# A new lead-in, loads in another order and one explicit emission order, in a kernel of layernorm, local attention and feed-forward

## The chip, the cores and the metric

One core of one Trainium2 chip. The metric is the device time of one execution in microseconds (us). Differences here are about one per cent, so each kernel was run several times beside runs of the kernel before on the same chip. Not all calls ran on the same chip, and there is one trace of each run. "Span" is the time from the first to the last record of the one execution that was profiled; it is about 2 us shorter than that execution's device time.

## The reference

A block of 2048 rows of 640 numbers: layernorm, then attention and feed-forward beside each other, all added to the input. Each row attends to 8 rows, itself and 7 earlier ones two apart.

```python
xn = _layernorm(x)
# attention: 32 heads of 20; logits over 8 offsets 0, 2, ..., 14 back
qkv = (xn @ wqkv) ...
logits = einsum("bhsd,bhswd->bhsw", q, kg) * scale      # kg: 8 shifted copies of k
o = einsum("bhsw,bhswd->bhsd", softmax(logits), vg)
# feed-forward 640 -> 1536 -> 640
h = gelu(xn @ w1 + b1)
return x + o @ wo + (h @ w2 + b2)
```

## The kernel before

The rows are cut into four chunks of 512, a chunk into four blocks of 128. Products with weights run on TensorE. The elementwise q times k and attention times v run on VectorE (32 passes of each, 1.48 us a pass). ScalarE empties TensorE's accumulator banks ("evictions") and does gelu and exp. Every piece of work has a name: `st10` is the statistics of chunk 1, block 0; `rs1` the root for all of chunk 1; `hc..`, `gc..` and `pc..` evict q, k, v; `qk..` are products of q and k, `lg..` the logits, `xs`/`xd` the DMAs that spread the attention weights (tile `ax`), `av..` their products with v, `ot` their sum, `f1`/`ge` the feed-forward with its gelu, `o...` output products, `oc`/`od` their eviction and the add into the output in memory. Each engine runs its pieces in the order in which they are emitted.

In the kernel before, that order comes out of a small greedy model that is run while the kernel is built:

```python
for eng in (PE, VE, SE, DQ):            # the plan's clock moves on; each free engine takes
    best = None                         # the ready piece of the lowest rank
    for t in left:
        if any(n not in end or end[n] + ... > now for n in t["needs"]):
            continue
        if any(len(held[p]) + k > self.pools[p] for p, k in new.items()):
            continue
        best = t
    ...
for t in make_plan(fns).run():          # pieces in order of their planned start
    t["fn"]()
```

Of the kernel before, what the change touches and what calls it, by code (L numbers as in the profile page):

```python
# [10 lines left out]
ACT = mybir.ActivationFunctionType  # L11
# [4 lines left out]
PE, VE, SE, DQ = "pe", "ve", "se", "dq"  # L16


class Plan:
# [8 lines left out]
    LAG = {PE: 0.22, VE: 0.08, SE: 0.1, DQ: 0.0}  # L28
# [4 lines left out]

    def pool(self, name, n):
        self.pools[name] = n

    def add(self, name, engine, us, rank, needs, fn, bufs=(), after=0.0, table=None, slack=0.0):
        t = {
            "name": name,
            "eng": engine,  # L40
            "us": us,
            "rank": rank + self.offsets.get(name[: 4 if name[:2] in ("pj", "pc", "ad") else 3], 0.0),
            "needs": list(needs),
            "fn": fn,
            "bufs": list(bufs),
            "after": after,
            "table": table,
            "slack": slack,
            "i": len(self.tasks),
        }  # L50
        self.tasks.append(t)
        self.by[name] = t
        for b in bufs:
            self.bufs.setdefault(b, set()).add(name)
        return name

    def run(self):
        end, left, held = {}, list(self.tasks), {p: {} for p in self.pools}
        remaining = {b: set(u) for b, u in self.bufs.items()}
        free = {PE: 0.0, VE: 0.0, SE: 0.0, DQ: 0.0}  # L60
        now, started, table = 0.0, [], "sqrt"
        running, slacks = [], {t["slack"] for t in self.tasks}
        while left:
            done = [t for t in running if t["end"] <= now + 1e-9]
            for t in done:
                running.remove(t)
                for b in t["bufs"]:
                    remaining[b].discard(t["name"])
                    if not remaining[b]:
                        held[b[0]].pop(b, None)  # L70
            moved = True
            while moved:
                moved = False
                for eng in (PE, VE, SE, DQ):
                    if free[eng] > now + 1e-9:
                        continue
                    best = None
                    for t in left:
                        if t["eng"] != eng or t["after"] > now + 1e-9:
                            continue  # L80
                        if best is not None and (t["rank"], t["i"]) >= (best["rank"], best["i"]):
                            continue
                        if any(
                            n not in end
                            or end[n] + t["slack"] + (self.LAG[self.by[n]["eng"]] if self.by[n]["eng"] != eng else 0.0) > now + 1e-9
                            for n in t["needs"]
                        ):
                            continue
                        new = {}
                        for b in t["bufs"]:  # L90
                            if b not in held[b[0]]:
                                new[b[0]] = new.get(b[0], 0) + 1
                        if any(len(held[p]) + k > self.pools[p] for p, k in new.items()):
                            continue
                        best = t
                    if best is not None:
                        left.remove(best)
                        best["start"], best["end"] = now, now + best["us"]
                        if best["table"] not in (None, table):
                            table = best["table"]  # L100
                            best["end"] += self.TABLE
                        end[best["name"]] = best["end"]
                        free[eng] = best["end"]
                        for b in best["bufs"]:
                            held[b[0]][b] = True
                        running.append(best)
                        started.append(best)
                        moved = True
            nxt = [f for f in free.values() if f > now + 1e-9]
            for late in slacks:  # L110
                ready = [e + late + self.LAG[self.by[n]["eng"]] for n, e in end.items()]
                nxt += [r for r in ready if r > now + 1e-9]
            nxt += [t["after"] for t in left if t["after"] > now + 1e-9]
            if left and not nxt:
                raise RuntimeError("no piece can start: " + ", ".join(t["name"] for t in left[:8]))
            if left:
                now = min(nxt)
        return started
# [3 lines left out]
P = 128  # L122
# [8 lines left out]
EPS = 1e-5  # L131
MASKED = -1e9
# [4 lines left out]
GROUPS = (((0, 0, 4),), ((1, 0, 4),), ((0, 4, 5), (1, 4, 5)), ((2, 0, 4),), ((2, 4, 5),))  # L137
# [3 lines left out]
RANK = {  # L141
    "av1": 36.4, "av2": 74, "f12": 4.1, "f13": 69.4, "gj1": 19.4, "gj2": -19.4, "o02": -8.9, "o10": 15.3,
    "o12": -3.3, "o13": -11.3, "o20": 117, "o31": 57.5, "o33": 85.2, "ot0": 20, "pj22": -106.4, "pj31": -13.1,
    "qk1": -4.8, "qk2": 4.4, "st2": 164.2, "st3": 219.3, "xn0": -14.7,
}


def make_plan(fns, offsets=RANK):

    pl = Plan(offsets)  # L150
    for name, n in (
        ("acc", 4), ("L", 1), ("O", 1), ("xnT", 3), ("q", 2), ("k", 2), ("v", 2), ("prod", 4),
        ("e", 1), ("attn", 1), ("ax", 1), ("oT", 1), ("hT", 18), ("osb", 2), ("xn", 2), ("m", 1), ("rs", 1), ("ss", 1),
    ):
        pl.pool(name, n)
# [3 lines left out]

    def done(n, which):  # L160
        if n:
            return [f"pc{n}{which}{to}" for to in range(KT)]
        return [f"gc{bl}{g}" for bl in range(BPC) for g, parts in enumerate(GROUPS) if which in [p[0] for p in parts]]

    pl.add("b1", VE, 0.1, -90, [], f("b1"), after=21.0)
    for n in range(NCH):
# [6 lines left out]
        for bl in range(BPC):  # L173
            land = (4.0, 4.0, 9.6, 9.6)[bl] if n == 0 else (0.0, 13.3, 17.1, 17.1)[n]
            r = -40 if n else -99
            pl.add(f"st{n}{bl}a", VE, 0.5, r, [], f("st", n, bl, 0), after=land)
            pl.add(f"st{n}{bl}", VE, 0.62, r, [f"st{n}{bl}a"] + ([f"rc{n}{bl - 1}"] if n == 0 and bl else []), f("st", n, bl, 1))
            if n == 0:
                pl.add(f"rs{n}{bl}", SE, 0.35, -99, [f"st{n}{bl}"], f("sqrt", n, bl, bl + 1), table="sqrt")
                pl.add(f"rc{n}{bl}", VE, 0.17, -99, [f"rs{n}{bl}"], f("rstd", n, bl, bl + 1))  # L180
# [3 lines left out]
        for bl in range(BPC):  # L184
            xn, tp = ("xn", n, bl), ("acc", "tp", n, bl)
            if n > 0:
                pl.add(f"xn{n}{bl}", SE, 0.81, early + -4.0, [f"rc{n}"], f("xn", n, bl), [xn])
                pl.add(f"tc{n}{bl}", DQ, 4.0 if n > 1 else 2.7, early - 3.0, [f"xn{n}{bl}"], f("td", n, bl), [xn, xnT], 21.5)
                continue

            for i, (a, b) in enumerate(((0, 2), (2, KT)) if bl == 0 else ((0, KT),)):
                u = "a" if b < KT else ""
                us = (b - a) / KT
                pl.add(f"xn{n}{bl}{u}", VE, 0.06 + 0.36 * us, -99, [f"rc{n}{bl}"], f("xn", n, bl, a, b), [xn])
                pl.add(f"tp{n}{bl}{u}", PE, (0.54 if bl == 0 else 0.3) * us, -99, [f"xn{n}{bl}{u}"], f("tp", n, bl, a, b), [xn, tp])
                pl.add(f"tc{n}{bl}{u}", SE, 0.16 + 0.49 * us, -99, [f"tp{n}{bl}{u}"], f("tc", n, bl, a, b), [tp, xnT])
        if n == 1:
            pl.add("ld", DQ, 9.2, -1000, [f"tc1{bl}" for bl in range(BPC)], f("ld"))
        pl.add(f"xp{n}", DQ, 0.3, base + 30, ["ld"], f("xp", n))
        pl.add(f"xb{n}", DQ, 0.0, base + 33, [f"xp{n}"], f("xb", n))  # L200

        if n == 0:
            for bl in range(BPC):
                for g, parts in enumerate(GROUPS):
                    ps, last = ("acc", "g", bl, g), max(p[0] for p in parts)
                    tos = sum(p[2] - p[1] for p in parts)
                    land = (6.4, 8.7, 11.8)[last]
                    r = -50 + (last == 2)
                    need, cut = [f"tc0{bl}"], 0
                    if bl == 0 and g == 0:  # L210
                        cut = 2
                        need.append(pl.add("ga00", PE, 0.112 * tos, r, ["tc00a"], f("gj", bl, g, 0, cut), [xnT, ps], land))
                    pl.add(f"gj{bl}{g}", PE, 0.056 * (KT - cut) * tos, r, need, f("gj", bl, g, cut, KT), [xnT, ps], land)
# [544 lines left out]
```

## Time and profile before

| what | before |
|---|---|
| device time, median of 3 (range) | 215.14 us (214.96 to 215.17) |
| span of the profiled execution | 212.4 us |
| first real product on TensorE | 7.03 us |
| last product done | 209.65 us |
| from there to the end ("tail") | 2.75 us |
| VectorE, ScalarE busy | 82%, 52% |

Read it as three stretches: up to the first product, the time in which TensorE is nearly always busy, and the tail. The profile's lines are in the prediction below. In this trace TensorE waits once for another engine after its filler, 0.46 us just before the first product.

### The profile page before, as it was taken

How to read it: one execution, taken by the hardware profiler on the slowest of the kernel's cores; microseconds unless marked ns; L12 is line 12 of the kernel's file. 1: busy time of each engine (PE TensorE's matmuls, PEld its weight loads, DVE VectorE, ACT ScalarE, POOL GpSimd, SP SyncE). 2: the span in 40 equal slices, each digit the busy share in tenths (PEclk: the TensorE clock that was granted, in tenths of full speed). 3: DMA queues.
4: the chain of work that ended last, by engine and by line, in shares of the span. 5: the costliest groups of instructions: out<-in, count | busy, mean ns of one | idle time of the engine just before them, and what ended most of it. 6: DMA issues, size and time to landing. Idle time of an engine off the chain costs nothing.

```text
span 212.4 us, 3961 instructions
## 1 busy us (share of the span) xinstructions
PE 206.9 (97%) x1670; PEld 121.7 (57%) x1693; DVE 174.4 (82%) x178; ACT 109.5 (52%) x193; POOL 19.7 (9%) x37
## 2 busy tenths in 40 slices
PE   8999999999999999999999999999999999999994
PEld 8799845655545555555555555455555455555552
DVE  3579999759999997599996999999999999972001
ACT  3568997798574654931353883503752511341120
POOL 2000000000020024101100010101110011101130
PEclk9999999999999999999999999999999999999999
DMA  6999528916829199993120027202114611122214
GB/s 216 365 362 376 93 50 275 322 24 132 206 64 163 37 287 196 197 195 89 15 30 0 0 31 200 31 3 31 14 21 48 180 19 22 27 29 31 34 16 76
DMA packets 23465, 23.95 MB, mean 113 GB/s; under 512 B 9112, under 2 KB 20632, under 8 KB 23448
## 3 DMA queue, kind: packets, MB, share of 16 engines
q1 hardware_dynamic: 17864, 16.49, 28.3%
q0 software_dynamic: 4144, 4.92, 17.2%
q10 hardware_dynamic: 1440, 2.29, 3.9%
q8 instruction: 13, 0.21, 0.4%
q14 instruction: 4, 0.03, 0.1%
HBM read 10.00 MB, written 7.54 MB: 83 GB/s over the span
## 4 chain that ended last, share of the span: by engine, by line
PE 97%; issue 1%; DVE 0%; ACT 0%
PE lo L684 27%; PE hps L653 24%; PE pps L484 23%; PE gps L501 8%; PE hi L686 8%; PE L L557 4%; PE idle L725 2%; PE tp L437 1%; ACT xnT L441 0%; DVE osb L714 0%; DVE zeros L361 0%
## 5 line engine op out<-in xcount | busy, mean ns | idle before, releaser
L653 PE MATMUL hps<-xnT,w_sb 128*128 128x512 bf16 x235 | 54.1, 379 | 0.3
L684 PE MATMUL lo<-w_sb,hT 128*128 128x512 bf16 x183 | 51.8, 379 | 0.0
L631 DVE TENSOR_TENSOR pv<-vT,ax 128x2560 bf16<-128x2560 bf16 x32 | 45.9, 1484 | 1.7 <-PE L L557 1.7
L535 DVE TENSOR_TENSOR prod<-qT,kT 128x2560 bf16<-128x2560 bf16 x32 | 45.4, 1484 | 0.0
L686 PE MATMUL hi<-w_sb,hT 128*128 128x128 bf16 x192 | 40.3, 219 | 0.6 <-issue 0.2
L664 ACT ACTIVATE hT<-hps,b1T 128x512 bf16<-128x512 f32 x48 | 31.6, 687 | 17.0 <-PE hps L653 13.3
L653 PEld LDWEIGHTS <-w_sb 128*128 128x128 bf16 x240 | 23.0, 98 | 26.7
L640 DVE TENSOR_TENSOR pv<-pv 128x5120 bf16<-128x5120 bf16 x12 | 33.9, 2825 | 0.4
L684 PEld LDWEIGHTS <-hT 128*128 128x128 bf16 x192 | 18.7, 98 | 22.8 <-issue 0.6
L691 ACT CAST osb<-lo 128x512 bf16<-128x512 f32 x15 | 8.8, 585 | 44.0 <-issue 28.0
L697 POOL DMA_DIRECT2D out_dram<-osb x15 | 12.9, 863 | 110.5 <-ACT osb L692 110.5
L684 PE MATMUL lo<-wo,oT 128*128 128x512 bf16 x79 | 23.0, 379 | 0.0
L686 PEld LDWEIGHTS <-hT 128*128 128x128 bf16 x192 | 18.4, 98 | 1.5
L398 DVE BATCH_NORM_STATS2 stats<-x_sb 128x6 f32<-128x320 bf16 x32 | 14.0, 469 | 5.1 <-DMA x_sb<-in_A_x_dram 5.1
L484 PE MATMUL pps<-xnT,wq_sb 128*128 128x512 bf16 x71 | 16.9, 380 | 0.2
L484 PE MATMUL pps<-xnT,wv_sb 128*128 128x512 bf16 x73 | 16.9, 379 | 0.1
L686 PE MATMUL hi<-wo,oT 128*128 128x128 bf16 x80 | 16.9, 219 | 0.1
L484 PE MATMUL pps<-xnT,wk_sb 128*128 128x512 bf16 x73 | 16.8, 379 | 0.1
L705 DVE TENSOR_TENSOR osb<-lo,x_sb 128x512 bf16<-128x512 f32 x1 | 0.7, 692 | 16.1 <-PE lo L684 16.1
L520 ACT CAST qT<-pps 128x512 bf16<-128x512 f32 x15 | 8.8, 585 | 9.2 <-PE pps L484 9.2
L684 PEld LDWEIGHTS <-oT 128*128 128x128 bf16 x80 | 7.8, 98 | 9.4
L484 PEld LDWEIGHTS <-wk_sb 128*128 128x128 bf16 x75 | 8.7, 118 | 7.3 <-issue 0.2
(62 smaller groups left out, 205.9 us busy)
## 6 DMA issues: line engine op xcount, KB each, us to landing
w_sb<-in_B_w_dram SPq DMA_DIRECT2D x2, 1920.0 KB, 9.2
out_dram<-osb POOLq DMA_DIRECT2D x15, 160.0 KB, 3.4
ax<-attn SPq DMA_DIRECT2D x8, 256.0 KB, 5.4
ax<-attn ACTq DMA_DIRECT2D x8, 256.0 KB, 5.6
out_dram<-x_sb SPq DMA_DIRECT2D x3, 640.0 KB, 4.3
out_dram<-b2bc POOLq DMA_DIRECT2D x3, 640.0 KB, 8.2
x_sb<-in_A_x_dram SPq DMA_DIRECT2D x1, 1280.0 KB, 13.3
wq_sb<-in_A_wqkv_dram SPq DMA_DIRECT2D x1, 800.0 KB, 4.8
```

The costliest lines, as they stand in the source:

```text
L398: nc.vector.bn_stats(stats[:, i, :], x_sb[:, b, i * (D // 2) : (i + 1) * (D // 2)])
L484: nc.tensor.matmul(ps[:], lhsT=wqkv_p[which][:, ti, to, :], rhs=xnT[:, ti, :], start=(ti == 0), stop=(ti == KT - 1),)
L501: nc.tensor.matmul(ps[:, i, :], lhsT=wqkv_p[which][:, ti, to, :], rhs=tiles["xnT", 0][:, ti, cs], start=(ti == 0 and (i == 0 or b == KT an ...
L520: nc.scalar.copy(dest[:, to, off : off + CH], tiles["pps", n, which, to][:])
L535: nc.vector.tensor_tensor(out=prod[:, i, :, :], in0=qkv_tile(n, 0)[:], in1=qkv_tile(n, 1)[:, :, off : off + CH], op=ALU.mult,)
L631: nc.vector.tensor_tensor(out=pv[:, i, :, :].rearrange("p t (j c) -> p t j c", j=BPC), in0=qkv_tile(n, 2)[:, :, off : off + CH].rearrange( ...
L640: nc.vector.tensor_tensor(out=ta[:], in0=ta[:], in1=tb[:], op=ALU.add)
L653: nc.tensor.matmul(ps[:], lhsT=w1_sb[:, ti, ft * P : (ft + 1) * P], rhs=tiles["xnT", n][:, ti, :], start=(ti == 0), stop=(ti == KT - 1),)
L664: nc.scalar.activation(hT[:], tiles["hps", n, ft][:], ACT.Gelu_apprx_tanh, bias=b1T[:, ft : ft + 1], scale=1.0)
L684: nc.tensor.matmul(lo[:], lhsT=lhs, rhs=rhs[:, 0:CH], start=first, stop=last)
L686: nc.tensor.matmul(hi[:, 0 : D - CH], lhsT=lhs, rhs=rhs[:, CH:D], start=first, stop=last)
L697: nc.gpsimd.dma_start(rows, tiles["osb", n, bl][:], accum_op=ALU.add)
```

## The change

Its intent is to start TensorE's real work earlier and to replace the greedy order by one that was searched offline. Block 0 is loaded alone, block 1 a little later (its load waits for a tiny fill on VectorE); block 1's statistics move to ScalarE; q, k and v of chunk 0 are made for pairs of blocks, 256 columns at a time (q of the first pair stays at 128); the transposed copies are shared between VectorE and ScalarE. w1 is loaded in two halves ahead of the last x. And the order of all pieces is one fixed list. Smaller edits are not shown, among them that the filler products read a constant and so start at 0.78 and not 0.99 us, and that the statistics get four buffers and not two. The core of the diff, cuts marked:

```diff
-    for cs in (slice(BPC, 2 * BPC), slice(2 * BPC, NCH * BPC)):
-        nc.sync.dma_start(x_sb[:, cs, :], x_nb[:, cs, :])
-    nc.sync.dma_start_transpose(b1_t[:], b1_rt[:])
-    nc.sync.dma_start(w1_sb[:], B_w1.rearrange("(t p) n -> p t n", p=P))
+    load_x(0, 1)
+    nc.vector.memset(x_sb[:, 1, 0:16], 0.0)
+    nc.scalar.dma_start(x_sb[:, 1, :], x_nb[:, 1, :])
...
+    load_x(BPC, 2 * BPC)
+    for c in range(2):
+        cs = slice(c * F // 2, (c + 1) * F // 2)
+        nc.sync.dma_start(w1_sb[:, :, cs], w1_v[:, :, cs])
+    nc.sync.dma_start_transpose(b1_t[:], b1_rt[:])
+    load_x(2 * BPC, NCH * BPC)
...
+    def do_sum1():
+        nc.scalar.activation(trash()[:], x_sb[:, 1, :], ACT.Identity, accum_out=acc1[:])
+    def do_sq1():
+        nc.scalar.activation(trash()[:], x_sb[:, 1, :], ACT.Square, bias=neg1[:], scale=RD, accum_out=mv[:, 1, 1:2])
...
+    def do_gp(which, pair, a, b):            # was: one block, 128 columns
+        for to in range(a, b):
+            for ti in range(KT):
+                nc.tensor.matmul(ps[:, to - a, :], lhsT=wqkv_p[which][:, ti, to, :],
+                    rhs=tiles["xnT", 0][:, ti, pair * 2 * P : (pair + 1) * 2 * P], ...)
...
+ORDER = """
+pad01 pad02 st00a st00 sm rs00 me nm rc00 sq xn00a xn00b tp00a tp00b tc00a rs01 ga tc00b rc01 xn01 gb2 tp01 gb3
...
+xn03 hc101 st12a tp02 st12 tp03 tc02 hj201 st10a tc03 st11a hj202 st11 hc200 hj010 st13a hc202 st13 hj011 st10 rs1
+hj110 hc010 rc1 hc011 hj112 xn10 hj111 hc112 hc110 hj012 xn11 hj210 hc012 hc111 st31a hj211 st22a hc210 tc11 qk020
+f107 hc211 hc201 b1 st20a f101 ge07 qk001 ...
...
+o233 ad31 ge31 o234 ge35 o330 oc23 o310 ad30 od23 o300 od13 o331 o301 ad32 o332 o302 o311 o312 ot3 o313 o303 o304
+o314 oc30 od30 o320 oc31 o321 od31 o322 o323 o324 o333 oc32 o334 od32 ohi oclo ochi
+""".split()
...
-        for t in make_plan(fns).run():
-            t["fn"]()
...
+        for name in ORDER:
+            pieces[name]["fn"]()
```

## The prediction

> **What bounds the kernel now.** I read the page first, then busy time by stretch, then TensorE in order of time over the first 25 us and the last 10, and last what VectorE and ScalarE did before TensorE's first real product. The page, its span, its engine row, and the chain that ended last:
>
> ```profile
> span 212.4 us, 3961 instructions
> ...
> PE 206.9 (97%) x1670; PEld 121.7 (57%) x1693; DVE 174.4 (82%) x178; ACT 109.5 (52%) x193; POOL 19.7 (9%) x37
> ...
> PE 97%; issue 1%; DVE 0%; ACT 0%
> ```
>
> TensorE carries 97% of the chain, so time can come only from TensorE doing less, starting earlier, or ending nearer the last byte. "Busy" isn't "at its peak", so I cut the span where TensorE's own timeline says its role changes: first real product at 7.03, first feed-forward product at 24.86, last product done at about 209.65. In the view of busy time by stretch (stretch, its length, PE busy, PEld, DVE, ACT, POOL, clock, DMA share, GB/s):
>
> ```profile
> 0.00:7.03 7.03, 5.58 (x49) 5.08 (x50) 2.98 (x10) 2.21 (x5) 1.46 (x18) 1.00 0.76 253
> 7.03:24.86 17.83, 17.83 (x315) 17.62 (x315) 14.26 (x43) 13.74 (x35) 0.00 (x0) 1.00 0.97 317
> 24.86:209.65 184.79, 183.46 (x1309) 99.03 (x1330) 156.90 (x125) 93.50 (x156) 18.21 (x19) 1.00 0.45 88
> 209.65:212.40 2.75, 0.00 (x0) 0.00 (x0) 0.29 (x1) 0.00 (x0) 0.00 (x0) 1.00 0.20 60
> ```
>
> The body, 184.79 us, is what a better order could fill. Is it already full? Starts of neighbouring matmuls in this trace lie 0.2158 us apart at 512 columns and 0.0558 at 128. The body holds 240 feed-forward and 225 projection matmuls of 512 (465 x 0.2158 = 100.3), 272 output pairs of 512 and 128 (272 x 0.2716 = 73.9), and the logits: one group of 80 at 2.30 us and six of 40 at 1.20 (9.5). That is 183.7, so about 1 us is left in 184.79, and most of it is the hand-over into and out of the narrow logits tiles (about 0.1 each, 14 times), which any order has. Order alone can win almost nothing here; it can only lose. What remains is the first 25 us. TensorE there (start, length, engine, line, what):
>
> ```profile
> 0.99 4.87 PE L725 MATMUL idle<-zeros 128*128 128x128 bf16 x44 [0.99 <-DVE zeros L361]
> 5.80 0.77 PE L437 MATMUL tp<-ident,xn 128*128 128x128 bf16 x5
> 7.03 1.28 PE L501 MATMUL gps<-xnT,wq_sb 128*128 128x128 bf16 x20 [0.46 <-ACT xnT L441]
> ...
> 22.07 2.95 PE L501 MATMUL gps<-xnT,wv_sb 128*128 128x128 bf16 x50
> 24.86 1.46 PE L653 MATMUL hps<-xnT,w_sb 128*128 128x512 bf16 x5
> ```
>
> The 44 products of zeros are filler; work begins at 7.03. What it waits for, on VectorE and ScalarE:
>
> ```profile
> 3.71 0.89 DVE L398 BATCH_NORM_STATS2 stats<-x_sb 128x6 f32<-128x320 bf16 x2 [2.77 <-DMA x_sb<-in_A_x_dram]
> 4.87 0.30 ACT L404 ACTIVATE std<-mv,eps_t 128x1 f32<-128x1 f32 x1 [2.18 <-DVE mv L400]
> 6.61 0.75 ACT L441 COPY xnT<-tp 128x256 bf16<-128x256 bf16 x2 [1.44 <-PE tp L437]
> 19.84 0.93 ACT L420 ACTIVATE xn<-x_sb,nmr,rstd 128x640 bf16<-128x640 bf16 x1
> x_sb<-in_A_x_dram SPq DMA_DIRECT2D x1, 160.0 KB, 2.9
> x_sb<-in_A_x_dram ACTq DMA_DIRECT2D x1, 160.0 KB, 3.1
> ```
>
> The reader is to see a chain of small steps: landing 3.68, statistics 3.71, root 4.87, first product 7.03. It is 3.32 us from landing to product and 2.16 from root to product. The fourth line is there only as the price of one ScalarE pass over a 640-wide block.
>
> **What the Trainium skill says.** "TensorE: Matmul & The Clock Gate", section "Back-to-back issue gap", gives N/2.4 + 2.5 ns per warm matmul: a fixed part beside the columns. The trace agrees: 50 products of 128 take 24.86 - 22.07 = 2.79 us, 55.8 ns each. By the same formula one of 256 takes 109.2 ns, against 111.6 for two of 128. The same page, Part 1 ("The HAM clock gate"), says that the array starts at half clock and needs about 3.4 us of work. Here the filler still ran at 107 ns a start up to 5.5 us, and the products at 7.03 at 56, so the filler is needed and its length barely suffices. "DMA: Bandwidth & Descriptors", section "Issuing engines are not separate DMA queues", says that loads from different engines share the same 16 engines and interleave. The trace agrees: the first two x loads, issued together, landed together, 2.9 and 3.1 us after issue.
>
> **The change, part by part.**
> (1) Block 0 alone first. The load of block 1 now waits for a tiny VectorE fill (in the kernel before, VectorE's first fill ran at 0.82 to 0.94), so it is issued near 1.05 and not 0.75. Block 0 has the engines to itself for that 0.3 us. I estimate that it lands 0.3 earlier, at 3.35, and block 1 at about 3.95 and not 3.86.
> (2) Block 1's statistics go to ScalarE: a sum pass, a negated mean, a square pass. In ScalarE's order the sum pass stands before block 0's root. It costs about 0.8 to 0.9 (the 0.93 row, less overlap). If block 1 lands at 3.6 the pass ends at about 4.4, when the statistics of block 0 are just done (3.35 + 1.16 = 4.5), and the root starts at 4.5. If block 1 lands at 3.95, the root starts at about 4.85, where it was. So the first product comes at 4.5 + 2.16 = 6.66 or at about 7.0. The first copy of the transposed block moves to VectorE, which frees the second for ScalarE at the same time; that is worth 0.1 at most for the products after the first ten. I take 6.6 for the first product: a gain of 0.4.
> (3) Pairs of blocks. The 300 lead-in products of 128 become 50 of 128 and 125 of 256: the same columns and 125 fewer matmuls. 50 x 0.0558 + 125 x 0.1092 = 2.79 + 13.65 = 16.44, against 300 x 0.0558 = 16.74: 0.3 saved, all on the bound engine.
> (4) The stretch from 7.03 holds 17.83 us, of which 16.74 are products and 15 transposes are 0.84. About 0.25 are small stalls. The new sequence keeps one such place (the first halves of block 1 wait for the VectorE copy), so I count 0.1 won.
> (5) Loads of w1 in halves before x of the last two chunks, and the order of output adds: all of it is off TensorE's path (w1 landed at 23.16 before, just ahead of its use at 24.86; now earlier). 0.
> (6) The end. Before, 17 products of 512 and 17 of 128 follow the last full block (3.67 + 0.96 us); now part of them is done earlier and only 8 of 512 and 17 of 128 follow (1.73 + 0.95). The last GpSimd add was issued about 1.04 after its block ended and landed 3.58 later, so it now lands about 1.9 to 2.0 us after TensorE's end, where the last small store landed 1.84 after it. I count 0.1 lost.
> (7) The fixed order in the body: 0, with the risk below.
> Sum: 0.4 + 0.3 + 0.1 - 0.1 = 0.7 us won of 215.14, so 214.4.
>
> **The rivals.**
> (a) Block 1 delays block 0: the sum pass holds the root, and after the root the square pass holds the other half of block 0's transposed copy. For it: ScalarE runs in order, and only 0.1 to 0.4 us of room is there. Against it: nothing but the small size of the delay. Then (1) and (2) give 0 or even -0.3, and the time is 214.8 to 215.2.
> (b) The fixed order stalls TensorE in the body. Tightest is the last attention chunk. By sums of trace durations, its logits end near 162 us; maximum, subtraction, exponential, sums, reciprocal and product (1.2 + 1.2 + 1.06 + 1.4 + 0.95 + 1.22, with hand-overs 7.2) bring 169.2; spreading the weights takes up to 6.3, 175.5; eight products of 1.43, three additions of 2.82 and the last addition of 1.49 bring 196.9. TensorE asks for it near 198.6. So there are some 1.7 us of room, where the kernel before had its result at 192.7 and asked for it at 195.89: 3.2 us. A late stage would cost a stall of its lateness. For it: VectorE is 82% busy. Against it: at every other place that I summed the room is 2 us or more. This would make 214.5 to 216.
> (c) The lead-in meets the landings: key weights landed at 8.59 and value weights at 11.75 before; the new order asks for them at about 10 and 12.7. The loads before them are the same bytes in the same order, so I don't expect it; a miss would cost under 0.5.
> (d) The whole gain is larger: block 0 alone lands 0.6 earlier, all handshakes shorten, and the time is 213.6.
>
> **Range and chances.** Faster by 2% would need 4.3 us. All of the time outside the full body is 7.03 + 2.75 us, and the change touches a part of the first. Slower by 2% would need stalls of 5 us at waits where I count 1.7 us of room or more. So "within 2%" is nearly sure. (a) and a small (b) set the upper end at 215.3, (d) the lower at 213.5.
>
> **What would show it right or wrong.** The statistics of block 0 should start near 3.35, the root near 4.5 to 4.85, the first real product at 6.5 to 7.0, with 256-column products 0.109 apart after it. Counting one projection product group of 0.55 that is left for later, feed-forward should start near 23.4. TensorE idle and stretched pitch after that should sum to no more than in the kernel before. I am wrong in step (2) if the root doesn't move, in (7) if the matmuls of the output projection in the last chunk wait for the attention result, and in (6) if the span ends more than 2.9 us after TensorE. The prediction as a whole fails if the time falls outside 213.5 to 215.3.

## More of the kernel before

The loads at the start, the lead-in's products and the two DMA queues that spread attention weights:

```python
nc.sync.dma_start(x_sb[:, 0, :], x_nb[:, 0, :])            # block 0
nc.scalar.dma_start(x_sb[:, 1, :], x_nb[:, 1, :])          # block 1
... wq, wk, x blocks 2-3, wv, b1 row ...
for cs in (slice(BPC, 2 * BPC), slice(2 * BPC, NCH * BPC)):   # x of chunk 1, x of chunks 2-3
    nc.sync.dma_start(x_sb[:, cs, :], x_nb[:, cs, :])
nc.sync.dma_start_transpose(b1_t[:], b1_rt[:])
nc.sync.dma_start(w1_sb[:], ...)                              # all of w1

def do_xd(n):
    expand(nc.sync, n, (0, 1))         # ax, from the sync queue
def do_xs(n):
    expand(nc.scalar, n, (2, 3))       # ax, from ScalarE's queue: a piece in ScalarE's order
```

## The result

The changed kernel took 217.37 us, median of 4 (216.51 to 218.96); the kernel before, beside it, 215.13 (214.96 to 215.17). The ratio is 1.0113, with a 95% interval of 1.0072 to 1.0154. Ratios in this text are the mean time of one kernel's fast runs over that of the other's of the same rounds, so not quite the ratio of the medians. It is within 2%, but slower, and outside the range of 213.5 to 215.3.

The page of the changed kernel: span, TensorE's row, and the chain that ended last by engine.

```profile
span 215.6 us, 3729 instructions
...
PE 208.0 (96%) x1568; PEld 121.4 (56%) x1568; DVE 174.2 (81%) x178; ACT 109.5 (51%) x192; POOL 19.7 (9%) x37
...
DVE 47%; PE 29%; DMA 15%; ACT 3%; issue 2%; SPq 2%; ACTq 0%; DVEq 0%
```

The 125 matmuls did go (the page before counted 1670 of its 1693, some records being missing). But where the chain before was 97% TensorE, 47% of it now is VectorE and 15% DMA: followed back from the end, the path leaves TensorE. That is the first sign of a wait that counts. The stretches, cut at the same events as before (stretch, length, busy PE, PEld, DVE, ACT, POOL, clock, DMA share, GB/s):

```profile
0.00:6.19 6.19, 5.24 (x49) 5.09 (x50) 2.44 (x10) 3.98 (x10) 1.46 (x18) 1.00 0.72 238
6.19:24.08 17.89, 16.89 (x186) 16.71 (x185) 8.79 (x29) 11.15 (x24) 0.00 (x0) 1.00 0.94 317
24.08:211.75 187.67, 185.90 (x1336) 99.62 (x1333) 162.65 (x140) 94.37 (x159) 18.29 (x19) 1.00 0.45 88
211.75:215.62 3.87, 0.00 (x0) 0.00 (x0) 0.29 (x1) 0.00 (x0) 0.00 (x0) 0.77 0.39 79
```

Against before, the first stretch lost 0.84 us (7.03 to 6.19). The second is 0.06 longer, though one group of v products (0.55) has left it for the third. The third grew by 2.88, the tail by 1.12: -0.84 + 0.06 + 2.88 + 1.12 = 3.22, the difference of the spans. So the start was won, more than predicted, and several times that was lost later. The view of waits for TensorE names the stops (who waited for whom: us in total, times, longest):

```profile
PE L L598 <- DVE prod L576: 1.3, 2, 0.7
...
PE gps L546 <- ACT qT L556: 1.0, 1, 1.0
...
PE hps L694 <- ACT hT L705: 0.5, 1, 0.5
```

In order of time they stand at 18.7 (1.0 us), 29.1 (0.5) and 162 to 164 (twice 0.65). By the starts of neighbouring matmuls they cost a little more, 1.16, 0.62 and 1.54, since a matmul's record ends some 0.15 after the next one could start. With the 0.55 that moved in, 0.62 + 1.54 + 0.55 = 2.71 of the third stretch's growth of 2.88 is placed; 0.17 is not; the 1.16 is hidden in the second, which would else have shrunk.

**The start.** ScalarE's root for block 0 and TensorE's first product:

```profile
4.46 0.29 ACT L423 ACTIVATE std<-mv,eps_t 128x1 f32<-128x1 f32 x1
...
6.19 1.00 PE L515 MATMUL gps<-xnT,wq_sb 128*128 128x128 bf16 x15 [0.17 <-DVE xnT L463]
```

The root came 0.41 earlier than before (4.87), as the step asked, and the way from root to product shrank from 2.16 to 1.73, because VectorE's copy of 0.29 replaced a ScalarE pass. Block 1's sum on ScalarE, which rival (a) feared, began at 3.62 and took 0.74 and a read of 0.19; it was done by 4.45, and the root followed at 4.46.

**Stop 1, at 18.7.** VectorE's first statistics of chunk 1; ScalarE's root for chunk 1 and the eviction behind it:

```profile
14.75 0.89 DVE L402 BATCH_NORM_STATS2 stats<-x_sb 128x6 f32<-128x320 bf16 x2 [2.24 <-DMA x_sb<-in_A_x_dram]
...
18.89 0.30 ACT L423 ACTIVATE std<-mv,eps_t 128x4 f32<-128x4 f32 x1 [3.05 <-DVE mv L404]
19.10 1.05 ACT L556 CAST qT<-gps 128x512 bf16<-128x512 f32 x2
```

The list has `st10 rs1 hj110 hc010 rc1 hc011 hj112`. ScalarE stands still for 3.05 us at the root `rs1`, which waits for the last statistics of chunk 1. The two evictions behind it have long had their data; TensorE wants the banks that they will free. The Trainium skill says of this ("PSUM — Partial Sum Buffer", section "Engine vs sequencer instructions") that the queues of ScalarE, VectorE and GpSimd are strict FIFO; the trace agrees, with ready evictions behind 3.05 us of waiting. The x of chunk 1 landed at 14.73 here and at 13.56 in the first trace of the kernel before. Are the w1 halves, which are now issued behind that load, to blame? No: with the old load order, in the first experiment below, it landed at 14.56, and another execution of the kernel before landed it at 14.67.

**Stop 2, at 29.1.** VectorE and ScalarE ahead of the first gelu, then the sync queue's issues:

```profile
23.71 0.89 DVE L402 BATCH_NORM_STATS2 stats<-x_sb 128x6 f32<-128x320 bf16 x2 [4.11 <-DMA x_sb<-in_A_x_dram]
...
25.90 0.17 DVE L584 CAST b1T<-b_t 128x12 f32<-128x12 bf16 x1
26.14 1.28 ACT L705 ACT_TABLE_LOAD   x1 [0.79 <-DVE b1T L584]
```

```profile
4.95 3.81 SPq L353 DMA_DIRECT2D w_sb<-in_B_w_dram  x2
...
13.34 0.57 SPq L337 DMA_DIRECT2D x_sb<-in_A_x_dram  x1
```

The last x (1280 KB) was issued at 13.34 and landed at 23.68. The sync queue first had to issue the transpose of b1, which waits for the b1 row until 11.7. In the kernel before, this load went out straight behind chunk 1's, the two issues done by 6.5, and landed at 18.25; w1 took the late place, where nothing in front of TensorE waited for it. In the list, VectorE has two statistics of that x ahead of its first q times k, and the copy of b1 that the gelu needs behind that. So VectorE stood still for 4.11 us, began q times k at 24.51 and not at 23.02, and the gelu came late.

**Stop 3, at 162.** Its cause lies 30 us earlier. The issues of the `ax` loads of chunk 2 in the changed kernel, an eviction between them, and VectorE's first use:

```profile
123.48 1.21 SPq L656 DMA_DIRECT2D ax<-attn  x2
...
125.73 0.58 ACT L561 CAST qT<-pps 128x512 bf16<-128x512 f32 x1 [1.33 <-PE pps L502]
125.90 0.55 ACTq L656 DMA_DIRECT2D ax<-attn  x1
...
133.23 8.50 DVE L672 TENSOR_TENSOR pv<-vT,ax 128x2560 bf16<-128x2560 bf16 x6 [2.58 <-DMA ax<-attn]
```

The same issues in the kernel before:

```profile
126.89 1.19 SPq L615 DMA_DIRECT2D ax<-attn  x2
127.03 2.24 ACTq L615 DMA_DIRECT2D ax<-attn  x2
```

Both queues wait for the same tile, the weights that VectorE finished at 123.46 (1.23 us from 122.23). The sync queue issued at once, ScalarE's queue 2.42 us later, since in ScalarE's order evictions stand ahead of it that wait for TensorE. In the kernel before the two queues issued 0.14 apart. Also, after three additions the searched order asks for `ax`, while the one before had eight q times k products to do first. VectorE waited 2.58 us; from 133.23 on it ran without a pause to the last chunk's products of q and k, so it could not catch up, and TensorE waited for them. The late issue is not the whole of it: the last of the four loads went out at 126.49 and landed at 133.15, and ahead of it the sync queue had sent a store of x into the output (480 KB, 124.73 to 132.02).

**The tail.** Last output add by GpSimd and last small store in the changed kernel, then in the kernel before:

```profile
210.14 0.86 POOL L738 DMA_DIRECT2D out_dram<-osb  x1 [3.76 <-ACT osb L733]
...
212.11 0.36 ACTq L758 DMA_DIRECT2D out_dram<-osb  x1
```

```profile
206.09 0.86 POOL L697 DMA_DIRECT2D out_dram<-osb  x1 [0.50 <-ACT osb L692]
...
210.00 0.36 ACTq L717 DMA_DIRECT2D out_dram<-osb  x1
```

The last add was issued 3.55 us ahead of TensorE's end before, 1.61 now. It landed at 213.58 (before: 209.67, ahead of the last small store). The last small store took from 212.11 to 214.28, 2.17 us, against 1.49 before. The other traces agree (the first try at the end, below, aside): the tail is 2.7 to 2.8 us in the four with the old end of the list and 3.1 to 3.9 in the nine with the changed end.

### The profile page after: what moved, and what is told of

It reads as the page before. It is cut to its first block, busy times and chain, and to the rows that moved or that the text cites. A ratio compares the mean times of both kernels' runs of the same rounds, so it can differ in the third digit from the quotient of the medians.

```text
span 215.6 us, 3729 instructions
## 1 busy us (share of the span) xinstructions
PE 208.0 (96%) x1568; PEld 121.4 (56%) x1568; DVE 174.2 (81%) x178; ACT 109.5 (51%) x192; POOL 19.7 (9%) x37
## 4 chain that ended last, share of the span: by engine, by line
DVE 47%; PE 29%; DMA 15%; ACT 3%; issue 2%; SPq 2%; ACTq 0%; DVEq 0%
DVE pv L672 15%; PE lo L725 14%; DVE prod L576 13%; DVE pv L681 10%; PE hps L694 8%; DMA ax<-attn 7%; DMA x_sb<-in_A_x_dram 5%; DMA b_rt<-in_B_b_dram 4%; PE hi L727 4%; PE pps L502 2%; DVE attn L646 2%; PE L L598 1%; DVE rs L641 1%; DVE z L618 1%; DVE m L611 1%
## 5 line engine op out<-in xcount | busy, mean ns | idle before, releaser
L694 PE MATMUL hps<-xnT,w_sb 128*128 128x512 bf16 x240 | 57.2, 379 | 0.5 <-ACT hT L705 0.5
L725 PE MATMUL lo<-w_sb,hT 128*128 128x512 bf16 x192 | 54.7, 379 | 0.0
L705 ACT ACTIVATE hT<-hps,b1T 128x512 bf16<-128x512 f32 x48 | 30.6, 687 | 20.6 <-PE hps L694 15.2
L694 PEld LDWEIGHTS <-w_sb 128*128 128x128 bf16 x240 | 22.3, 98 | 25.9 <-issue 1.5
L402 DVE BATCH_NORM_STATS2 stats<-x_sb 128x6 f32<-128x320 bf16 x30 | 13.0, 467 | 10.1 <-DMA x_sb<-in_A_x_dram 10.1
L502 PE MATMUL pps<-xnT,wv_sb 128*128 128x512 bf16 x75 | 18.0, 379 | 0.0
L502 PE MATMUL pps<-xnT,wk_sb 128*128 128x512 bf16 x75 | 17.5, 379 | 0.0
L502 PE MATMUL pps<-xnT,wq_sb 128*128 128x512 bf16 x75 | 17.4, 379 | 0.0
L483 POOL DMA_DIRECT2D out_dram<-b2bc x4 | 5.3, 1324 | 89.0 <-DMA out_dram<-x_sb 89.0
L502 PEld LDWEIGHTS <-wq_sb 128*128 128x128 bf16 x75 | 8.7, 118 | 7.5 <-issue 0.4
```

The costliest lines, as they stand in the source:

```text
L402: nc.vector.bn_stats(stats[:, i, :], x_sb[:, b, i * (D // 2) : (i + 1) * (D // 2)])
L483: nc.gpsimd.dma_start(dst, b2bc[:].unsqueeze(1).to_broadcast([P, cs.stop - cs.start, D]), accum_op=ALU.add)
L502: nc.tensor.matmul(ps[:], lhsT=wqkv_p[which][:, ti, to, :], rhs=xnT[:, ti, :], start=(ti == 0), stop=(ti == KT - 1),)
L694: nc.tensor.matmul(ps[:], lhsT=w1_sb[:, ti, ft * P : (ft + 1) * P], rhs=tiles["xnT", n][:, ti, :], start=(ti == 0), stop=(ti == KT - 1),)
L705: nc.scalar.activation(hT[:], tiles["hps", n, ft][:], ACT.Gelu_apprx_tanh, bias=b1T[:, ft : ft + 1], scale=1.0)
L725: nc.tensor.matmul(lo[:], lhsT=lhs, rhs=rhs[:, 0:CH], start=first, stop=last)
```

## The experiments

All kernels give the right result. Where an edit only moves names in the list, the diff shows the names. The theory after reading the traces: the loads' order and three places in the list (root of chunk 1, statistics of the late x, `ax` issues on ScalarE's queue) cost the time, and the end a part. The main rivals: the order as a whole is at fault, or the stops hide one another so that removing one gains nothing.

### Only the loads put back

```diff
     load_x(BPC, 2 * BPC)
-    (w1 in halves; transpose of b1)
     load_x(2 * BPC, NCH * BPC)
+    (transpose of b1; w1 whole)
```

> The changed kernel with only its load order set back: x of the last two chunks straight after x of the second chunk, then the bias transpose, then w1 whole. Theory L (late x loads cost the time): x of the second chunk lands near 13.6 and not 14.73, the last x near 18.3 and not 23.68; the 1.16 us stall before the key pair goes, VectorE's 4.11 us wait goes, the first q*k product starts near 22.9 and not 24.5, the stall of 1.5 us at the last chunk's logits shrinks to under 0.5; w1 lands near 23.2, which costs up to 0.4 at the first feed-forward product. Time 214.5 to 215.3. Theory O (the fixed order of the body is too tight by itself): the logits stall stays near 1.5 and the time is 216.2 or more. The tail of about 3.8 us from TensorE's end to the span's end stays in both.

Measured: 215.51 us median (215.29 to 217.29), ratio to before 1.0012 [0.9968, 1.0055]. The last x landed at 18.24, q times k began at 23.23, stop 2 was gone, and stop 3 shrank to 0.2 although nothing was done to it. Stop 1 was expected to go and stayed at 0.6: x of chunk 1 landed at 14.56 and not at 13.6. So the load order costs about 2 us of the loss (217.37 in an earlier call, to 215.51), more than the 0.62 of its own stop. How the rest comes about is read from the table further below.

A caution for this and the next three runs: four of eleven runs of the kernel before took 216.7 to 217.0 us, the others 214.84 to 215.65. All count, and they make every ratio of this call some 0.3% smaller than in the others.

### The new lead-in with the old loads and the old body order

```diff
-ORDER = (as in the changed kernel)
+ORDER = (the changed kernel's pieces up to the end of the lead-in, then all others
+         as the greedy model of the kernel before had ordered them)
     (loads as in the experiment above)
```

> The new lead-in (pieces of block 0 to 3 in their new form and order), the load order of before, and the order of the kernel before for everything else. If the new lead-in is worth what its own start and matmul count say (start 0.84 earlier, 0.55 less work), TensorE ends near 208.3 and not 209.65, the tail is 2.75 as before, and the time is 213.6 to 214.1. If the lead-in is itself at fault, the time is 215 or more.

Measured: 214.31 us (214.16 to 215.65), 0.9946 [0.9907, 0.9985]: faster than the kernel before. So the lead-in's gain is real and reaches the end if the rest is left alone. Its own start is not always what the first trace of the changed kernel had: in the eleven traces with the new lead-in the first product came at 6.19 to 7.21 (median 6.31), and in four of them it waited 0.21 to 1.05 us for q's weights. The profiled execution was the slowest of the six, and shows why single executions can lie 1.4 us off:

```profile
6.87 1.77 PE L513 MATMUL gps<-xnT,wq_sb 128*128 128x128 bf16 x15 [0.71 <-DMA wq_sb<-in_A_wqkv_dram]
```

These 15 products took 1.77 us, where the changed kernel's row above has 1.00: in this execution the first 28 products, with 5 transposes among them, started up to 107 ns apart, until 10.35 us: 3.48 us for 33 starts, where 33 x 0.056 are 1.85, so 1.6 us more. The Trainium skill ("TensorE: Matmul & The Clock Gate", Part 1) says that the cold time varies from run to run, as the activity window is free-running; this execution agrees.

### The old lead-in and loads with the searched body order

```diff
-for t in make_plan(fns).run():
+for name in ORDER:     # old lead-in pieces, then the changed kernel's order of all others
+    pieces[name]["fn"]()
     (and four buffers for statistics, not two, which that order needs)
```

> The reverse: lead-in and loads of the kernel before, and the searched order for everything else. Theory O: a stall of 1 us or more at the last chunk's logits and a tail of 3.8 us, time 217 or more. Theory L alone: no stall in the body, but the tail still 1 us longer, time near 216.2. If the searched body is harmless in both, 215.1.

Measured: 215.97 us (215.73 to 217.78), 1.0026 [0.9984, 1.0068]. By the interval alone this is unclear. The time is near what theory L alone asked for, but the trace shows theory O's stop at the logits (1.0 us in the view of waits) and a tail of 3.39, without the new loads. The pair "only the loads put back" against "new lead-in, old body" differs only in the list after the lead-in: 215.51 against 214.31, 1.2 us. So the searched order costs about 1.2 us by itself, where I had predicted none. Its end is part of that: the tails of the two traces are 3.42 and 2.75.

### Only the statistics of the late x moved behind the first q times k

```diff
-... hc111 st31a hj211 st22a hc210 tc11 qk020 f107 hc211 hc201 b1 st20a f101 ... qk011 ld ...
+... hc111 hj211 hc210 tc11 qk020 f107 hc211 hc201 b1 f101 ... qk011 st31a st22a st20a ld ...
```

> The changed kernel with its new load order kept; only three statistics of the late x blocks move in VectorE's order from ahead of the first q*k products to after them. If VectorE's wait for the late x is what delays the body, the q*k products start 1.1 us earlier (23.4), the bias is cast earlier, the 0.6 us stall near 28.8 goes and the logits stall falls from 1.5 to about 0.4; the 1.16 us stall stays; time 215.7 to 216.3. If the wait does not matter, 217.4 as before.

Measured: 216.14 us (215.62 to 216.72), 1.0018 [0.9978, 1.0058]. VectorE's first q times k:

```profile
23.30 1.49 DVE L576 TENSOR_TENSOR prod<-qT,kT 128x2560 bf16<-128x2560 bf16 x1 [3.79 <-ACT kT L556]
```

It no longer waits for the x but for k itself, and starts 1.2 us earlier; stop 2 is gone. By the medians about 1.2 us comes back, with the loads left as the change has them. So a good part of the harm of the load order went through VectorE's place in the list, not through TensorE missing data. The expectation had stop 3 falling to 0.4; it stayed (0.63 and 0.67), though VectorE had begun its products as early as with the old loads.

### The changed kernel again, and the root of chunk 1 two evictions later

The repeat serves as the base of the next two:

> The changed kernel unchanged, beside the other edits on one chip, because its four runs spread over 2.4 us. If what its first trace showed is the rule, the time is 216.5 to 217.8, with the last x landing near 23.7, the first q*k product near 24.5 and a logits stall of over 1 us in the last chunk.

It took 217.88 us (216.98 to 220.17), 1.0141 [1.0104, 1.0178], with the same shares in the chain that ended last (47% VectorE). Stops 2 and 3 are there again (0.47; 0.81 and 0.68), the last x landed at 23.58, and q times k began at 24.41. But stop 1 is not there. TensorE began a microsecond later, waiting for q's weights, and met no wait at 18.7:

```profile
7.21 1.03 PE L515 MATMUL gps<-xnT,wq_sb 128*128 128x128 bf16 x15 [1.05 <-DMA wq_sb<-in_A_wqkv_dram]
```

```diff
-... st10 rs1 hj110 hc010 rc1 hc011 hj112 ...
+... st10 hj110 hc010 hc011 rs1 rc1 hj112 ...
```

> The changed kernel with one ScalarE piece moved: the root of the second chunk (and the reciprocal after it) comes after two PSUM evictions in place of before them. TensorE's 1.16 us stall before the second half of the key pair should go in any case. If VectorE's chain from the late x to the last logits sets the end (theory L with a VectorE-bound body), TensorE only waits longer at the logits and the time stays within 0.4 us of the changed kernel's. If the stall itself is on the path to the end, the time falls by 0.8 to 1.2 us.

Measured: 216.75 us (216.24 to 217.95), 1.0091 [1.0069, 1.0114]: 1.1 us less than the repeat beside it. ScalarE now has the eviction ahead of the root:

```profile
17.93 0.59 ACT L556 CAST qT<-gps 128x512 bf16<-128x512 f32 x1 [0.51 <-PE gps L546]
18.75 0.30 ACT L423 ACTIVATE std<-mv,eps_t 128x4 f32<-128x4 f32 x1 [0.23 <-DVE mv L404]
```

Stop 1 is gone and stop 2 remains (0.68). The gain has the size of stop 1, as the expectation said, but it is not made there (and the two intervals just overlap). At 37 us TensorE is only 0.14 us ahead of the first trace of the changed kernel and 0.03 ahead of the repeat: at stop 2 it waits for the same late gelu. What is gone too is stop 3, which this edit was not meant to touch:

```profile
162.01 1.57 PE L598 MATMUL L<-prod,head_of 128*32 128x256 bf16 x40
```

So that stop 1 costs time is not shown by this run, and the time agreeing with one of the two expectations is luck.

### All `ax` loads of chunks 0 and 2 from the sync queue

```diff
-        expand(nc.sync, n, (0, 1))
+        expand(nc.sync, n, (0, 1) if n % 2 else range(BPC))
...
-        expand(nc.scalar, n, (2, 3))
+        if n % 2:
+            expand(nc.scalar, n, (2, 3))
```

> The changed kernel with the attention weights of chunks 0 and 2 spread by four loads on the sync queue in place of two there and two on ScalarE's queue, where they stood behind evictions and were issued 2.4 us late. If that lateness is a second cause of the logits stall, the last of chunk 2's four loads is issued near 125.3 and not 126.5, VectorE's wait for them (2.58 us) falls by 1 to 2, the logits stall by as much, and the time by 1 to 1.5 us (215.9 to 216.4). If the loads are held by bandwidth and not by their issue, nothing changes (217).

Measured: 216.09 us (216.01 to 216.21), 1.0053 [1.0040, 1.0066]: 1.8 us less than the repeat. TensorE's logits of the last chunk run as one group, without a stop:

```profile
161.93 1.32 PE L598 MATMUL L<-prod,head_of 128*32 128x256 bf16 x40
```

VectorE still waited for `ax` of chunk 2, but 1.78 us and to 131.48, not to 133.23. The last issue came at 125.05, as expected; the wait shrank by 0.8 only, where 1 to 2 was expected. The bytes are the same; only the queue of issue differs, and with it the place of two loads, now ahead of the store of x and not behind it. That the edit helps is shown by the time. How much of it is the late issue is not, as the traces side by side tell (starts in us; one trace of each run):

| what starts | changed | again | root later | `ax` from sync | statistics later | loads put back |
|---|---|---|---|---|---|---|
| VectorE: first q times k | 24.51 | 24.41 | 24.37 | 24.29 | 23.30 | 23.23 |
| TensorE: first k of chunk 1 | 37.12 | 37.01 | 36.98 | 36.89 | 36.41 | 36.33 |
| VectorE: first `av` of chunk 1 | 103.27 | 103.22 | 102.21 | 102.33 | 102.06 | 101.52 |
| VectorE: first `av` of chunk 2 | 133.23 | 133.54 | 131.82 | 131.48 | 132.51 | 131.27 |
| TensorE: first logits of the last chunk | 155.42 | 155.32 | 155.28 | 155.20 | 154.71 | 154.64 |
| stop 3, sum of the waits | 1.31 | 1.49 | 0 | 0 | 1.30 | 0.20 |
| TensorE: last product done | 211.75 | 212.17 | 210.41 | 210.07 | 211.19 | 209.80 |

From 37 to 155 us TensorE runs in step in all six; what stops 1 and 2 leave is settled by then. Stop 3 follows VectorE's first `av` of chunk 2: at 132.5 and later it is there, at 131.9 and earlier it is nearly or quite gone. Most of that time VectorE gains at its two waits for `ax`. With the loads put back its lead of 1.28 us at the start is 0.78 by 54 us and 1.75 after the wait of chunk 1. With the root later and with `ax` from the sync queue, 0.7 to 1.0 of it is gained at chunk 1, whose loads neither edit touches (the last landed at 103.09 and 102.93 in the two traces of the changed kernel, at 102.03 and 102.15 in these). Whether the edits bring these earlier landings or chance does is not shown. The late issue alone doesn't make stop 3: with the loads put back and with the root later ScalarE's queue issued 3.3 to 3.4 us behind the sync queue, and the stop was 0.2 or gone.

### The lead-in and old body, with the root of chunk 1 later

The lead-in experiment above plus the root's move, as the best guess at a version that beats both:

> The new lead-in with the load order and the body order of the kernel before, as in the earlier run of that kind, and the root of the second chunk moved behind two evictions. It should lose the short stall before the key pair (0.5 to 0.8 us where x of the second chunk lands after 14): 213.5 to 214.0 against 214.3; if the body before was waiting elsewhere anyway, 214.3.

Measured: 213.93 us (213.85 to 214.53), 0.9959 [0.9946, 0.9971], against 215.05 for the kernel before beside it. This is the fastest version, 1.1 us under the kernel before and almost 4 under the changed one of the same call. Its page row for the engines and its middle stretch:

```profile
PE 207.2 (98%) x1568; PEld 120.5 (57%) x1568; DVE 174.1 (82%) x178; ACT 110.1 (52%) x191; POOL 19.7 (9%) x37
```

```profile
24.07:209.06 184.99, 184.95 (x1331) 98.88 (x1328) 158.54 (x126) 94.38 (x158) 18.23 (x19) 1.00 0.46 89
```

TensorE is busy for 184.95 of 184.99 us; the changed kernel had 185.90 of 187.67 there. Whether the root's move adds to the lead-in experiment is not settled, since the two ran in different calls and their intervals overlap.

### Three repairs to the changed kernel

Old loads, root later, `ax` from the sync queue, the rest of the searched order kept:

> The changed kernel with the three corrections together: the load order of before, the second chunk's root behind two evictions, the weights of chunks 0 and 2 spread from the sync queue. If the three stalls (1.16, 0.62 and 1.5 us) are the whole loss in TensorE's run, TensorE has no stall over 0.3 us left, ends near 208.7, and the time is 214.3 to 214.9: about 0.8 above the new lead-in with the old body, which would be the tail. If the searched body costs more than that, 215.3 or more.

Measured: 214.55 us (214.48 to 215.29), 0.9979 [0.9957, 1.0001]. So three small edits take the loss against the kernel before away, and their gains overlap: alone they gave about 1.9, 1.1 and 1.8, which is 4.8, and together 217.88 - 214.55 = 3.3. By the medians of two calls it stays some 0.6 above the version with the old body, by the ratios 0.4, and the intervals overlap. Its trace has a tail of 3.33, and one new stop of 0.56 at 199, where the last chunk's output waits for the attention result; but this execution was the slowest of the six, so I don't count that stop for the others.

### The kernel before, once more, with a profile

> The kernel before, run as these are, to have its trace and its time from one execution on this chip: time 215.1, TensorE's end 5 to 5.5 us before the time, as in the others; x of the second chunk landing at 13.4 to 14.6. No theory hangs on it.

Measured: 215.12 us (214.44 to 215.58), 0.9993. The x of chunk 1 landed at 14.67 here, against 13.56 in the first trace and 14.73 in the changed kernel; TensorE had one stop of 0.46 at 16.0. So that load's landing differs by 1.1 us between executions of one kernel. In the eleven traces with the new lead-in it landed at 14.06 to 14.73, whether w1 was behind it or not, so inserting w1 did not delay it.

### The end alone: a first try that tested something else

In the best version, the first nine output products of the last block moved ahead of blocks 12 to 14:

```diff
-o304 o312 oc30 o313 od30 o320 o321 o322 o323 o324 o314 oc32 od32 o330 oc31 o331 od31 o332 o333 o334 ohi oclo ochi
+o330 o331 o332 o304 o312 oc30 o313 od30 o320 o321 o322 o323 o324 o314 oc32 od32 oc31 od31 o333 o334 ohi oclo ochi
```

> The best kernel so far (new lead-in, old loads, old body, root behind two evictions) with one thing of the searched order put in: three pieces of the last block are done early, so that after the last full block 2.7 us of TensorE work are left and not 4.6. If that is what lengthens the tail, TensorE's end stays within 0.1 us, the last GpSimd add lands about 2 us after it, the span ends 3.4 to 3.8 us after it and not 2.74, and the time is 214.5 to 214.9 against 213.9. If the tail is long for another reason, 213.9.

Measured: 215.23 us (214.87 to 215.55), 1.0001 [0.9978, 1.0025]. TensorE ended at 209.03, as in its base, and the tail grew from 2.74 to 4.21. But VectorE's last addition shows another cause than in the changed kernel:

```profile
209.69 0.69 DVE L744 TENSOR_TENSOR osb<-lo,x_sb 128x512 bf16<-128x512 f32 x1 [17.60 <-DMA out_dram<-osb]
```

There are two output buffers. In my order the last block got the one of block 14, whose add, issued at 206.07, held it until 209.51. The changed kernel has no such wait, so this run doesn't explain its tail.

### The end alone, with the changed kernel's own last pieces

```diff
-o304 o312 oc30 o313 od30 o320 o321 o322 o323 o324 o314 oc32 od32 o330 oc31 o331 od31 o332 o333 o334 ohi oclo ochi
+o330 o331 o332 o304 o312 oc30 o313 od30 o314 o320 oc31 o321 od31 o322 o323 o324 o333 oc32 o334 od32 ohi oclo ochi
```

> The best version so far (new lead-in, old loads, old body order, root of chunk 1 later) with nothing changed but its last twenty pieces, which now stand as in the changed kernel: the first nine of the twelve feed-forward steps of the last block are done early, block 14 is the last whole block and its output add is issued while the last block is finished; the adds of blocks 12, 13, 14 are copied in that order, so that the last block's output buffer is the one of block 13 and not of block 14 (the mistake of the earlier tail run). Theory (the late GpSimd add makes the tail): TensorE's end stays at 209.0 to 209.3, the last GpSimd add is issued about 1.4 to 1.6 before TensorE's end and lands 3.4 later, the span ends 3.4 to 3.9 after TensorE (2.74 in the base), and the time is 214.6 to 215.0 (0.9 below or at the kernel before). Rival (the tail of the changed kernel has another cause, such as ScalarE being late there after the stalls): the tail stays at 2.7 to 3.0 and the time at 213.9 to 214.1. In no case do I expect VectorE's last output additions to wait for the output buffer.

Measured: 214.74 us (213.97 to 215.25), 0.9986 [0.9961, 1.0010], against 213.93 for its base, with the kernel before at 215.1 in both. So about 0.6 (by the ratios) to 0.8 us seems to come from these last pieces alone; the two runs are from different chips, and their intervals just overlap. The profiled execution was the fastest of the six. In it TensorE ended at 209.05, the last add was issued at 207.44 and landed at 210.53, no addition waited for a buffer, and the tail was 3.08: the last store took 1.77 us, against 1.48 in the base. The time is as the theory wanted, the tail of this one execution is between theory and rival. In the fourteen traces the last store took 1.48 to 1.49 us in the four where the last add had landed before it was issued, and 1.72 to 2.17 in the ten where it had not. That the add in flight is what slows the store is likely by this, but no run isolates it.

### All runs

| kernel | median (range), us | ratio to before, 95% |
|---|---|---|
| changed | 217.37 (216.51 to 218.96) | 1.0113 [1.0072, 1.0154] |
| changed, again | 217.88 (216.98 to 220.17) | 1.0141 [1.0104, 1.0178] |
| root later | 216.75 (216.24 to 217.95) | 1.0091 [1.0069, 1.0114] |
| statistics later | 216.14 (215.62 to 216.72) | 1.0018 [0.9978, 1.0058] |
| `ax` from the sync queue | 216.09 (216.01 to 216.21) | 1.0053 [1.0040, 1.0066] |
| old lead-in, searched body | 215.97 (215.73 to 217.78) | 1.0026 [0.9984, 1.0068] |
| loads put back | 215.51 (215.29 to 217.29) | 1.0012 [0.9968, 1.0055] |
| three repairs | 214.55 (214.48 to 215.29) | 0.9979 [0.9957, 1.0001] |
| new lead-in, old loads and body | 214.31 (214.16 to 215.65) | 0.9946 [0.9907, 0.9985] |
| the same, root later | 213.93 (213.85 to 214.53) | 0.9959 [0.9946, 0.9971] |
| that, with the changed end | 214.74 (213.97 to 215.25) | 0.9986 [0.9961, 1.0010] |
| that, first try at the end | 215.23 (214.87 to 215.55) | 1.0001 [0.9978, 1.0025] |
| before, again | 215.12 (214.44 to 215.58) | 0.9993 [0.9969, 1.0017] |

## Why the prediction was right or wrong

The class, within 2%, was right. The time of 214.4 and its range were wrong, and the sign with them.

In the first trace steps (1) to (3) held. Block 0's statistics started at 3.23 (predicted 3.35), the root at 4.46 (4.5), the first product at 6.19 (6.6; over the eleven traces the median is 6.31): the gain was 0.84 and not 0.4. The missing part is in step (2), where I priced the VectorE copy at 0.1 at most: root to product fell by 0.43. The 125 matmuls went. (One reading of the lines is off by a little: from landing to product it is 7.03 - 3.68 = 3.35 us; 3.32 counts from the statistics.)

Step (4), 0.1 won in the lead-in's small stops, failed: a stop of 1.16 came in. Rival (c), that the lead-in meets the landings, was the right family, but I put it aside because the bytes ahead of q, k and v are the same. It named weights of k and v. In the first trace what was asked for too early was the *statistics* of chunk 1, by a root standing in front of evictions; in the repeat it was the weights of q, and TensorE came out of stop 2 at nearly the same time (29.46 against 29.56). So a first product a microsecond earlier was worth nothing by 29 us.

Step (5) is the largest error: "all of it is off TensorE's path ... 0". The load order costs about 2 us. I asked whether w1 lands before TensorE needs it, and did not ask what lands later in exchange: the last x went from 18.25 to 23.68, and VectorE had been ordered to wait for it. Taking VectorE's wait away gave about 1.2 back, putting the loads back about 1.9.

Step (7), the fixed order in the body at 0, failed through rival (b), which I had named but with the wrong place. I took the last chunk's attention result as tightest, with 1.7 us of room, and claimed 2 us or more elsewhere. The logits of the last chunk had less than none: TensorE stood there for 1.31 us and 1.49 us in two traces, and the searched order costs 1.2 us with the same lead-in and loads. My sums took durations and left out that a DMA issue on ScalarE's queue is a piece of ScalarE's order; `ax` of chunk 2 was issued 2.4 us late from there. Issuing the loads of chunks 0 and 2 elsewhere gave 1.8 back, by way of earlier landings of which only a part is explained. Also, slack isn't local: a load of chunk 1 or 2 that lands late at 103 or 133 us is paid for at 162.

Step (6), the end, had the right sign and the wrong size: 0.1 predicted, 1.12 in the first trace, 0.6 to 0.8 by an experiment. I had the add landing 1.9 to 2.0 after TensorE's end, and 213.58 - 211.75 = 1.83 is what it did. The term that I missed is the small stores, whose last one took 2.17 us and not 1.49. What slows it is open.

The parts do not add up: 1.9, 1.1 and 1.8 alone, but 3.3 together. All three traces are without most or all of stop 3, so that stop is counted three times.

## What to carry to other kernels

When a fixed order replaces a greedy one, read each in-order engine for pieces that wait for something uncertain (a landing, another engine) while ready pieces stand behind them, and count a DMA issue among an engine's pieces. When a load moves forward, list what moves back, and look who waits for that, on any engine. And a reordering that saves bound-engine work should be tried with the rest of the order left alone: here the lead-in alone gained 0.4 to 0.5%, and the loads and the searched order took that and more away. And when an edit gains about what a stop cost, lay the starts of the same instructions side by side in both traces before believing that the gain was made at that stop.

## What the Trainium skill lacked or had wrong

- "DMA: Bandwidth & Descriptors", section "Issuing engines are not separate DMA queues": it says that issuing from several engines saves only the sequencer's time to initiate, usually small. It lacks the other side: an issue on ScalarE's queue stands behind that engine's evictions. Here it went out 2.42 us after the sync queue's for the same tile (125.90 against 123.48); issuing these loads of chunks 0 and 2 from the sync queue won 1.8 us; the share of the late issue in that is not isolated.
- "DMA: Bandwidth & Descriptors" gives no spread of landing times between executions that I found. The 640 KB of x for chunk 1 landed at 13.56 and 14.67 in two executions of the same kernel, about as much as stop 1 (1.16).
- "TensorE: Matmul & The Clock Gate", Part 1: it is right that the cold time varies by run, and that the cost is under 1% of a span. What it lacks is that under 1% can still hide a result: one execution lost 1.6 us that way, 0.8% of this kernel, as large as most of the differences tested here, so a single execution can't judge such a change.
- "TensorE: Matmul & The Clock Gate", section "Back-to-back issue gap": it calls the formula N/2.4 + 2.5 ns, which the prediction uses, that of an isolated matmul, and gives about 81 ns at 128 columns and 131 at 512 for a stream in a real kernel. Here the streams ran at 55.8 and 215.8 ns, as the formula has it.
- No page prices a small store at the end of a kernel beside an add still in flight: 1.72 to 2.17 us in ten traces against 1.48 to 1.49 in four, cause not isolated.
